# The first batch's k: transposed in float32 by TensorE instead of being cast to bf16 first, with a new instruction order

## The chip, the cores and the metric

The kernel runs on one core of one Trainium2 chip. A core has five engines that work side by side, each through its own queue in order: TensorE (PE in the profile, with its weight loads listed apart as PEld), VectorE (DVE), ScalarE (ACT), GpSimd (POOL) and SyncE (SP, which here only issues DMA transfers). Engines wait for one another by semaphores. PE reads its operands from SBUF and writes to PSUM, which has eight banks of 128 x 512 float32; the other engines copy the results out. The metric is the device time of one execution in microseconds (us), as the median of several runs. The cost of one instruction is best read from the distance between starts of neighbours, since the printed duration of a matmul or a copy contains a part that overlaps with the next.

## The reference: linear attention by random features, then a gated MLP

Inputs are q, k, v of shape (8 batches, 8 heads, 576 rows, 64), omega (128, 64), and two weights, w_in (512, 2048) and w_out (2048, 512), all float32. Cut to what is computed:

```python
def phi(x):                                   # x is q or k, scaled by 64 ** -0.25
    h = x @ omega.T - (x * x).sum(-1, keepdims=True) / 2
    return np.exp(h - h.max(-1, keepdims=True)) / np.sqrt(128)
q_p, k_p = phi(q), phi(k)                     # (8, 8, 576, 128)
kv  = einsum('bhsm,bhsd->bhmd', k_p, v)       # (8, 8, 128, 64)
z   = k_p.sum(2)
out = einsum('bhsm,bhmd->bhsd', q_p, kv) / (einsum('bhsm,bhm->bhs', q_p, z) + 1e-6)
x   = out.transpose(0, 2, 1, 3).reshape(4608, 512)
h   = x @ w_in                                # (4608, 2048)
y   = (h * clip(h + 3, 0, 6) / 6) @ w_out     # (4608, 512), float32
```

The kernel leaves out the factors that cancel between numerator and denominator: for k it divides the rows of v by the row maximum of the exponential, for q nothing is needed.

## The kernel before

**The work.** Attention goes batch by batch (`attention(b)`), heads in four pairs. Each of a batch's 576 rows splits into 512 main rows and 64 leftover rows. For a batch: transpose k and q so that the 64 features lie on partitions (`kT`, `qT`), project with omega on PE, take the exponential on ACT (`kp` for k, `qpT` for q), reduce a row maximum of `kp` on DVE (`mx`), invert it (`cc`), scale v by it (`vc`, `vcl`), multiply (`kv`, and its copy `kvz`), multiply with q's features (`num`), divide on DVE (`rec`, `div`) into `xb`, and transpose that into `xT` for the MLP. The MLP goes in blocks of 512 rows: `mm1` with w_in, the gate (a ReLU with scale and bias on ACT into `tsb`, then a minimum and a product on DVE into `gT`), `mm2` with w_out. Later blocks replace eight products by seven, with sums of operands made on POOL and DVE (names S, T, X, W). Block 0 runs through `mm1_half` in halves of 256 rows, each PE instruction group taking two of the sixteen feature groups of 128; its group 12 is the first to need the last quarter of w_in.

**The first batch.** Its rows of q, k, v are loaded as float32 by SP, with two of the k loads on ACT's queue. The main rows of k come in four pieces (two groups of head pairs, two heads of a pair). In the kernel before, each piece is cast to bf16 (`cast`: on ACT one piece, on POOL three) into `kb`; four PE transposes of 128 x 128 against a bf16 identity turn it into a PSUM bank (`turns`), and ACT or DVE copies 512 columns of bf16 out into `kT`. q is handled the same way. For batch 1 the load itself casts, on POOL's queue; from batch 2 on, DMA transposes.

**Filler.** So that PE is busy from the beginning, `idle_work` makes up to 76 matmuls of 256 columns that compute nothing (`fill`). The first 16 wait only for a memset; the others also for the first piece of k's main rows. The planner puts them where it sees PE idle, until 21 us of its own time.

**The order.** Nothing is scheduled on the chip. Every operation is recorded with `op(...)`: engine or choice of engines, a cost, reads and writes. The list `ORDER` at the head of the file gives, for each engine, the sequence of operations; it comes from a search outside the kernel, with a model of costs. `Prog.schedule` follows it, gives out PSUM banks and places the fillers; `Prog.emit` adds the semaphore waits. So an engine works strictly in the listed order, and a late operand stops what is queued behind it. The loads of w_in (five, cast to f16 by the DMA) and of w_out go through POOL's queue together with those of batch 1; SP's loads of v for batch 1 wait for the last piece of w_in.

**Lines.** In the profile of before, L571 fills the filler's operand and L576 is a filler matmul; L535 a transpose of k or q, L538 one of `xb`; L523 and L524 are copies and casts (523 on ACT, 524 on DVE and POOL); L811 projects k, L818 its exponential, L822 `mx`; L831 projects q, L835 its exponential; L850 and L935 invert the maximum; L941 and L943 make `vc` on POOL and on ACT, L857 and L860 `vcl`, L948 and L949 a column of `vc`; L957 and L959 are `kv`; L985 and L911 `num`, L997 and L1001 the division; L1199, L1054, L1133 and L1224, L1312 are matmuls of the MLP, L1208 and L1060 its ReLU, L1210 and L1062 its gate, L1328 sums out of PSUM; L622 loads q, k, v, and L595 and L604 load w_in and w_out.

Of the kernel before, what the change touches and what calls it, by code (L numbers as in the profile page):

```python
# [20 lines left out]
        13, 118, 139, 156, 124, 144, 150, 162, 115, 168, 147, 127, 153, 121, 159, 165, 136, 130, 133, 177, 185, 175,  # L21
        183, 197, 187, 142, 212, 179, 181, 199, 204, 214, 171, 227, 242, 202, 217, 229, 244, 219, 410, 416, 173, 189,
        417, 232, 404, 254, 247, 405, 222, 234, 406, 207, 249, 407, 257, 411, 412, 418, 413, 419, 422, 280, 425, 252,
        237, 260, 428, 300, 431, 434, 437, 440, 286, 284, 282, 443, 318, 306, 303, 288, 446, 449, 309, 312, 452, 298,
        296, 455, 315, 324, 294, 345, 458, 290, 575, 292, 321, 353, 576, 577, 327, 341, 335, 585, 586, 337, 339, 587,
        595, 588, 596, 331, 605, 366, 333, 578, 329, 579, 597, 355, 589, 590, 379, 598, 591, 368, 371, 592, 392, 580,
        581, 343, 606, 599, 381, 358, 607, 384, 600, 582, 394, 397, 601, 374, 608, 361, 609, 602, 387, 400, 610, 611,
        612, 638, 514, 626, 506, 629, 512, 623, 641, 632, 653, 504, 508, 499, 647, 644, 662, 656, 659, 484, 475, 487,
        496, 478, 481, 674, 668, 520, 518, 490, 493, 677, 510, 516, 671, 784, 785, 528, 502, 794, 533, 540, 530, 787,
        545, 542, 800, 564, 552, 788, 717, 554, 795, 569, 566, 557, 797, 798, 697, 801, 803, 804, 710, 807, 808, 811,  # L30
        817, 826, 724, 820, 737, 814, 832, 841, 829, 835, 739, 742, 749, 844, 847, 850, 761, 862, 856, 859, 773, 754,
        865, 778, 766, 751, 972, 988, 775, 973, 763, 982, 975, 976, 983, 885, 985, 986, 989, 898, 991, 992, 1005, 999,
        1014, 1002, 995, 996, 1017, 905, 1008, 1023, 1020, 1029, 925, 1035, 1032, 912, 1038, 1044, 937, 1050, 927,
        1047, 949, 1053, 939, 942, 930, 1160, 1161, 1176, 954, 961, 1170, 966, 951, 963, 1163, 1171, 1086, 1164, 1173,
        1174, 1073, 1177, 1179, 1180, 1093, 1202, 1193, 1190, 1187, 1183, 1184, 1100, 1205, 1196, 1113, 1208, 1217,
        1211, 1118, 1220, 1223, 1125, 1226, 1115, 1137, 1127, 1235, 1130, 1139, 1238, 1232, 1142, 1149, 1241, 1348,
        1349, 1151, 1364, 1154, 1351, 1274, 1352, 1358, 1359, 1281, 1365, 1361, 1362, 1390, 1375, 1378, 1381, 1367,
        1368, 1393, 1371, 1372, 1384, 1405, 1261, 1399, 1414, 1396, 1420, 1411, 1408, 1426, 1301, 1313, 1429, 1303,
        1318, 1306, 1536, 1315, 1423, 1325, 1537, 1288, 1552, 1539, 1540, 1327, 1546, 1330, 1547, 1462, 1337, 1549,
        1342, 1339, 1550, 1553, 1469, 1555, 1556, 1476, 1559, 1560, 1449, 1563, 1569, 1566, 1572, 1581, 1501, 1593,  # L40
        1506, 1503, 1489, 1584, 1525, 1494, 1578, 1491, 1530, 1527, 1513, 1587, 1518, 1596, 1515, 1599, 1602, 1614,
        1608, 1611, 1617, 1631, 1632, 1662, 1675, 1634, 1665, 1691, 1678, 1667, 1635, 1680, 1704, 1670, 1694, 1641,
        1720, 1696, 1683, 1642, 1707, 1699, 1723, 1709, 1733, 1644, 1645, 1725, 1712, 1749, 1736, 1650, 1738, 1728,
        1762, 1752, 1651, 1741, 1754, 1809, 1765, 1647, 1648, 1812, 1767, 1822, 1757, 1654, 1814, 1655, 1770, 1825,
        1817, 1838, 1827, 1778, 1779, 1841, 1851, 1830, 1843, 1867, 1781, 1854, 1782, 1846, 1856, 1880, 1870, 1788,
        1872, 1859, 1883, 1789, 1885, 1909, 1875, 1794, 1896, 1791, 1792, 1888, 1899, 1795, 1912, 1901, 1941, 1914,
        1797, 1798, 1904, 1917, 1801, 1935, 1925, 1926, 1802, 1936, 1928, 1929, 1938, 1939, 1942, 1960, 1957, 1945,
        1946, 1954,
    ],
    "SP": [  # L50
        0, 21, 17, 23, 19, 22, 25, 24, 31, 27, 32, 26, 28, 29, 30, 269, 270, 271, 474, 473, 472, 471, 470, 468, 690,
        469, 402, 614, 584, 694, 696, 594, 693, 695, 692, 604, 536, 548, 560, 572, 691, 573, 881, 878, 810, 883, 879,
        806, 745, 757, 781, 769, 882, 782, 880, 884, 1069, 998, 1072, 1066, 1070, 1071, 994, 1068, 933, 945, 970, 957,
        969, 1067, 1260, 1259, 1257, 1258, 1186, 1133, 1121, 1145, 1157, 1182, 1254, 1158, 1256, 1255, 1374, 1370,
        1447, 1445, 1446, 1448, 1309, 1443, 1333, 1321, 1345, 1444, 1346, 1442, 1509, 1497, 1533, 1521, 1562, 1558,
        1534, 1653, 1657, 1800, 1804, 1953, 1952, 1959, 1962, 1950, 1956,
    ],
    "ACT": [
        18, 20, 117, 119, 157, 145, 151, 163, 132, 169, 148, 129, 154, 193, 166, 196, 160, 178, 211, 184, 137, 176,
        186, 225, 182, 180, 243, 188, 172, 218, 174, 190, 223, 408, 414, 420, 423, 281, 426, 238, 208, 429, 253, 432,  # L60
        301, 435, 438, 441, 283, 285, 444, 261, 319, 307, 304, 447, 310, 450, 313, 289, 299, 352, 297, 325, 346, 316,
        453, 291, 293, 354, 322, 328, 342, 336, 338, 456, 340, 332, 378, 367, 334, 391, 330, 459, 390, 380, 344, 593,
        583, 362, 375, 388, 401, 613, 507, 515, 630, 627, 624, 513, 642, 633, 639, 654, 505, 509, 500, 648, 645, 603,
        663, 657, 660, 476, 497, 482, 479, 485, 675, 488, 494, 519, 669, 491, 523, 511, 672, 517, 503, 529, 539, 678,
        521, 551, 550, 553, 565, 720, 718, 723, 722, 706, 703, 704, 700, 708, 698, 403, 713, 711, 716, 715, 736, 709,
        812, 702, 748, 818, 747, 729, 821, 727, 815, 725, 730, 827, 833, 830, 836, 759, 842, 848, 845, 851, 863, 857,
        774, 860, 866, 974, 977, 897, 894, 891, 896, 892, 888, 886, 899, 890, 903, 921, 901, 1000, 1006, 1003, 923,
        1015, 1018, 906, 936, 904, 1009, 1024, 908, 1021, 911, 1030, 910, 1036, 1033, 913, 574, 915, 1039, 1045, 918,
        938, 1051, 1048, 917, 1054, 959, 960, 962, 1091, 1087, 1092, 1089, 1079, 1084, 1076, 1082, 1074, 1078, 1080,
        1085, 1098, 1099, 1094, 1096, 1194, 1191, 1108, 1203, 1188, 1112, 1111, 1206, 1103, 1197, 1105, 1101, 1209,  # L70
        1212, 1124, 1136, 1218, 1221, 1106, 1224, 1126, 1227, 1138, 1147, 1148, 1239, 1233, 1236, 1242, 1350, 1277,
        1280, 1279, 1275, 1284, 1287, 1282, 1376, 1353, 1379, 1391, 1382, 1286, 1312, 1394, 1385, 1406, 1262, 1270,
        1268, 1266, 1400, 1264, 1415, 1267, 1397, 1297, 1412, 1273, 1409, 1272, 1427, 1324, 1421, 1323, 1430, 1538,
        1424, 1293, 1291, 1289, 1541, 1336, 1294, 1338, 1468, 1465, 1463, 1467, 1474, 1472, 1470, 1159, 1475, 1479,
        1477, 1482, 1481, 1450, 1452, 1458, 1456, 1564, 1455, 1570, 1567, 1454, 1488, 1573, 1502, 1461, 1582, 1460,
        1490, 1585, 1526, 1579, 1514, 1594, 1588, 1597, 1603, 1600, 1609, 1615, 1612, 1618, 1633, 1663, 1664, 1676,
        1677, 1666, 1692, 1679, 1671, 1693, 1636, 1673, 1695, 1684, 1705, 1706, 1686, 1722, 1708, 1700, 1724, 1702,
        1713, 1734, 1735, 1715, 1750, 1737, 1729, 1731, 1753, 1763, 1742, 1764, 1744, 1758, 1810, 1813, 1823, 1760,
        1771, 1824, 1773, 1826, 1818, 1820, 1839, 1831, 1842, 1780, 1852, 1853, 1847, 1833, 1783, 1849, 1860, 1881,
        1882, 1862, 1884, 1876, 1878, 1897, 1889, 1891, 1900, 1913, 1905, 1918, 1907, 1920, 1927, 1930, 1948, 1949,  # L80
        1951,
    ],
    "DVE": [
        16, 12, 11, 15, 14, 5, 138, 4, 9, 140, 10, 125, 7, 158, 146, 116, 191, 152, 164, 6, 122, 128, 149, 155, 194,
        209, 134, 167, 170, 131, 161, 141, 239, 224, 198, 143, 200, 213, 201, 205, 215, 216, 228, 203, 206, 230, 245,
        231, 220, 246, 221, 233, 255, 248, 235, 236, 250, 258, 256, 251, 409, 415, 259, 421, 424, 8, 427, 1623, 430,
# [316 lines left out]
def _emit(nc, es, q, k, v, omega, w_in, w_out, out):  # L403
# [38 lines left out]
    def sbt(name, shape, dt):  # L442
        return es.enter_context(nc.sbuf_tensor(name, list(shape), dt))
# [166 lines left out]
    def mains_of(t):  # L610
        return t[:, NP:, :].rearrange("p (m h r) d -> p m h (r d)", h=2, r=4)
# [890 lines left out]
```

The softmax here doesn't subtract the row's maximum and nothing guards it: scores larger than these inputs give would overflow.

## Time and profile before

| | us |
|---|---|
| median of six runs | 303.89 (303.27 to 304.55) |
| the profiled execution's own time | 304.24 |
| its span, from first to last instruction | 302.40 |
| PE busy in the span | 295.75 |
| PE busy from 0 to 22 us, filler included | 19.73 |
| first real MLP matmul (L1199) | 20.6 |
| DMA, mean over the span | 148 GB/s |

The profiled execution took 0.35 us more than the median, and 1.84 us lie outside its span. In the profile, a line of the timeline gives start, length, engine, source line, operation and tiles, `xN` for N merged instructions, and in brackets the idle time before it with the engine or DMA that ended it. "Busy" for PE counts pipelined matmuls as they overlap, so 98% says that PE is rarely without an instruction, not that each is useful.

### The profile page before, as it was taken

What the parts mean: (1) busy time and instruction counts of PE and PEld (TensorE: products, weight loads), DVE (VectorE), ACT (ScalarE), POOL (GpSimd) and SP (SyncE); (2) the same over time, 40 slices, a digit from 0 to 9 for tenths busy, and PEclk for the clock granted to TensorE, in tenths of its full rate; (3) what the DMA queues carried; (4) which work ended last, traced back from release to release, by engine and by line L of the source; (5) the groups of instructions that cost most, each with busy time, mean ns of one, the idle gap of its engine ahead of it and who ended that gap; (6) DMA issues with size and microseconds to landing.
All of it is one profiled execution on the core that took longest, in us unless ns stands there. A gap on an engine that the chain in (4) does not pass through costs nothing.

```text
span 302.4 us, 7405 instructions
## 1 busy us (share of the span) xinstructions
PE 295.8 (98%) x2795; PEld 211.4 (70%) x2800; DVE 246.4 (81%) x547; ACT 214.2 (71%) x516; POOL 237.8 (79%) x255
## 2 busy tenths in 40 slices
PE   7999999999999999999999999999999999999995
PEld 5779955545776568655865586657756688888884
DVE  3889887859988794879878967687798999999875
ACT  4898996579949963799479854697686687575400
POOL 2883776069896999799969996998959999999990
PEclk9999999999999999999999999999999999999999
DMA  7999999999996996799949969797832500110034
GB/s 236 285 194 185 267 180 110 195 179 149 233 196 113 143 235 169 159 157 234 181 107 137 160 158 236 107 223 132 138 90 52 168 1 2 69 73 2 0 141 140
DMA packets 90100, 44.89 MB, mean 148 GB/s; under 512 B 57936, under 2 KB 87760, under 8 KB 90064
## 3 DMA queue, kind: packets, MB, share of 16 engines
q1 hardware_dynamic: 62496, 31.04, 45.4%
q0 software_dynamic: 26592, 12.46, 33.4%
q10 hardware_dynamic: 976, 0.92, 0.9%
q8 instruction: 22, 0.36, 0.5%
q14 instruction: 14, 0.11, 0.2%
HBM read 36.73 MB, written 9.44 MB: 153 GB/s over the span
## 4 chain that ended last, share of the span: by engine, by line
PE 87%; ACT 7%; DVE 5%; issue 0%
PE p L1312 32%; PE p L1054 24%; PE p L1133 8%; PE p L1224 5%; PE p L985 3%; PE p L1199 3%; PE p L957 3%; PE p L767 2%; ACT kp L818 2%; DVE gT L1062 2%; PE p L770 2%; PE p L576 1%; DVE mx L822 1%; ACT qpT L835 1%; PE p L831 1%; ACT tsb L1060 1%
## 5 line engine op out<-in xcount | busy, mean ns | idle before, releaser
L1054 PE MATMUL p<-xT,wi 128*128 128x512 f16 x384 | 89.9, 379 | 0.1
L1062 DVE SCALAR_TENSOR_TENSOR gT<-tsb,p 128x512 f16<-128x512 f16 x96 | 62.2, 676 | 12.8 <-ACT tsb L1060 12.2
L1060 ACT ACTIVATE tsb<-p 128x512 f16<-128x512 f32 x96 | 55.4, 606 | 14.7 <-PE p L1054 8.9
L1054 PEld LDWEIGHTS p<-xT,wi 128*128 128x128 f16 x384 | 35.7, 98 | 38.5 <-issue 1.1
L1312 PE MATMUL p<-wo,gT 128*128 128x256 f16 x368 | 45.3, 273 | 0.0
L1240 POOL TENSOR_TENSOR gT<-gT 128x512 f16<-128x512 f16 x32 | 36.9, 1155 | 3.2 <-DVE gT L1062 0.9
L1312 PEld LDWEIGHTS p<-wo,gT 128*128 128x128 f16 x368 | 35.0, 98 | 6.4 <-issue 1.1
L1240 POOL TENSOR_TENSOR s<-gT 128x512 f16<-128x512 f16 x31 | 36.2, 1168 | 3.9 <-DVE gT L1062 1.7
L1240 POOL TENSOR_TENSOR s<-gT,s 128x512 f16<-128x512 f16 x31 | 35.9, 1157 | 2.6 <-DVE gT L1062 0.3
L1240 POOL TENSOR_TENSOR gT<-gT,s 128x512 f16<-128x512 f16 x30 | 34.7, 1155 | 2.3
L791 DVE TENSOR_REDUCE mx<-kp 128x4 f32<-128x512 bf16 (+1 forms) x50 | 29.7, 621 | 6.5 <-ACT kp L786 6.4
L795 ACT ACTIVATE qpT<-p 128x512 bf16<-128x512 f32 (+1 forms) x50 | 27.5, 570 | 7.7 <-PE p L770 7.1
L622 POOL DMA_DIRECT2D qb<-in_q_dram x28 | 19.6, 716 | 16.7 <-PE p L1054 15.8
L1312 PE MATMUL p<-t,gT 128*128 128x256 f16 x256 | 31.6, 273 | 0.0
L786 ACT ACTIVATE kp<-p 128x512 bf16<-128x512 f32 (+1 forms) x50 | 26.2, 568 | 7.5 <-PE p L770 7.5
L941 POOL TENSOR_TENSOR vc<-v,cc 128x512 bf16<-128x512 f32 x22 | 24.0, 1089 | 8.8 <-DMA v<-in_v_dram 3.6
L1001 DVE TENSOR_TENSOR xb<-p,rec 128x256 f16<-128x256 f32 (+1 forms) x64 | 28.4, 470 | 0.3
L1312 PEld LDWEIGHTS p<-t,gT 128*128 128x128 f16 x256 | 24.4, 98 | 4.5 <-issue 1.6
L523 ACT COPY p<-p 128x256 f32<-128x256 f32 (+1 forms) x42 | 16.4, 402 | 14.9 <-PE p L1312 8.6
L1181 ACT ACTIVATE tsb<-p 128x512 f16<-128x512 f32 x32 | 18.7, 601 | 8.3 <-PE p L1133 6.2
L1183 DVE SCALAR_TENSOR_TENSOR gT<-tsb,p 128x512 f16<-128x512 f16 x32 | 21.1, 678 | 0.5 <-ACT tsb L1181 0.3
L943 ACT ACTIVATE vc<-v,cc 128x64 bf16<-128x64 f32 x80 | 20.2, 345 | 0.0
(132 smaller groups left out, 583.7 us busy)
## 6 DMA issues: line engine op xcount, KB each, us to landing
v<-in_v_dram SPq DMA_DIRECT2D x14, 512.0 KB, 5.4
out_dram<-osb SPq DMA_DIRECT2D x14, 512.0 KB, 3.7
kb<-in_k_dram POOLq DMA_DIRECT2D x14, 256.0 KB, 5.2
qb<-in_q_dram POOLq DMA_DIRECT2D x14, 256.0 KB, 5.9
wo<-in_moe_w_out_dram POOLq DMA_DIRECT2D x8, 256.0 KB, 9.5
wi<-in_moe_w_in_dram POOLq DMA_DIRECT2D x3, 512.0 KB, 7.4
q<-in_q_dram SPq DMA_DIRECT2D x4, 256.0 KB, 5.3
v<-in_v_dram SPq DMA_DIRECT2D x4, 256.0 KB, 5.6
```

The source lines that it names most:

```text
L786: op("ACT", actt(128 * (d1 - d0)), lambda E, lh=lh, ko=ko, part=part: E.activation(ko, out_of(part, 0, lh)[0].rearrange("p (x m) -> p x m" ...
L791: op("DVE", dvet(128 * (d1 - d0)), lambda E, ko=ko, mo=mo: E.reduce_max(mo, ko, axis=AX.X), p0 + 0.01, reads=[("kp", 0, d, lh) for d in ra ...
L795: op("ACT", actt(128 * (d1 - d0)), lambda E, lh=lh, part=part: E.activation(qd[:, part[0]:part[1], lh, :], out_of(part, 1, lh)[0].rearrang ...
L941: return E.tensor_tensor(vcm[:, :, 0:D], v32[:, m, :, :], cbc, ALU.mult)
L1001: op("DVE", dvet(128 * n), lambda E: E.tensor_tensor(xv(i0, i1), psum()[:, :, :, 0:64], rbc, ALU.mult), t + 0.01, reads=[vn, ("rec", ru)], ...
L1054: ins = E.matmul(ring.t[vh.slot], wi[:, c, 128 * f:128 * f + 128], xv[:, c, :], start=(c == 0), stop=(c == NJ - 1))
L1060: op("ACT", actt(512), lambda E: E.activation(tsb[tu][:], ring.t[vh.slot], AF.Relu, bias=0.5, scale=1.0 / 6.0), t - 0.1, reads=[vh], write ...
L1062: op("DVE", dvet(512), lambda E: E.scalar_tensor_tensor(gT[gu][:, f, :], tsb[tu][:], 1.0, ring.t[vh.slot], ALU.min, ALU.mult), t - 0.1, re ...
L1133: ins = E.matmul(dst, w(c), x[:, c, :], start=start and c == 0, stop=c == 1, skip_group_check=True)
L1183: op("DVE", dvet(512), lambda E, v=v, tu=tu, dst=dst: E.scalar_tensor_tensor(dst(), pieces(tsb[tu][:]), 1.0, pieces(v.ring.t[v.slot]), ALU ...
L1240: op(engines, {"POOL": 0.07 + n / 455.0, "DVE": 0.1 + n / 850.0}, lambda E: E.tensor_tensor(dst, x, y, ALU.subtract if minus else ALU.add) ...
L1312: ins = E.matmul(ring.t[v.slot][:, 256 * j:256 * j + 256], a[:, f, 128 * j:128 * j + 128], w[:, f, :], start=(first and f == 0 and j == 0) ...
```

## The change

The four casts of k's main rows in batch 0 are gone. PE transposes the float32 rows directly, against a float32 copy of the identity (a new 128 x 128 tile, made by one POOL copy), into a whole PSUM bank of float32. The copy out of PSUM writes bf16, so it does the rounding that the cast did. k's leftover rows and all of q still go through the cast. `ORDER` is replaced as a whole by a new sequence; the planner's rule for placing fillers is the same, and with the new sequence it places 49 instead of 65.

```diff
 ORDER = {
...
-    (five sequences)
+    (five other sequences)
...
     ident = sbt("ident", [128, 128], BF16)
+    identf = sbt("identf", [128, 128], F32)
...
+    op("POOL", 0.3, lambda E: E.tensor_copy(identf[:], ident[:]), -8.95, reads=["ident"], writes=["identf"])
     op("POOL", 0.3, lambda E: E.tensor_copy(identx[:], ident[:]), -8.9, reads=["ident"], writes=["identx"])
...
+        def turns32(t, name, dbl, dst, src, rd, p):
+            vT = Virt(ring)
+            n = 128 * len(dbl)
+
+            def e_T(E):
+                for i, x in enumerate(dbl):
+                    ins = E.transpose(ring.t[vT.slot][:, 128 * i:128 * i + 128],
+                                      src[:, 2 * x:2 * x + 2, :].rearrange("p c d -> p (c d)"), identf[:])
+                return ins
+
+            op("PE", len(dbl) * 0.23, e_T, p, reads=rd + ["identf"], writes=[vT], alloc=[vT], lat=0.25, name="T%s%d.%s" % (t, b, name))
+            op(T0, both(n), evac(lambda: dst, lambda: ring.t[vT.slot][:, 0:n].rearrange("p (j t) -> p j t", j=dst.shape[1])),
+               p, reads=[vT], writes=[(t + "T", x) for x in dbl], name="Tev%s%d.%s" % (t, b, name))
+
...
                 for hh in range(2):
                     nm = "%d%d" % (m0 // 2, hh)
                     dbl = four(m0, m1, hh)
-                    cast("k", nm, 512, mains_of(kb)[:, m0:m1, hh, :], mains_of(k32)[:, m0:m1, hh, :],
-                         main_keys("k", range(m0, m1), [hh]), dbl, 0)
-                    turns("k", nm, dbl, dbls(kT)[:, m0:m1, hh, :], kb, 0)
+                    turns32("k", nm, dbl, dbls(kT)[:, m0:m1, hh, :], k32, main_keys("k", range(m0, m1), [hh]), 0)
```

What the new sequence moves near the start, beside the change itself: `vc` of head pair 2 goes from ACT to POOL, the cast of k's leftover rows from DVE to POOL, one cast of q's main rows from ACT to DVE and that of q's leftover rows from DVE to ACT; on SP one k load comes one place later and one v load ahead of a q load; on POOL the first three loads of w_in are issued one after another. Later on, single copies and sums of the MLP change between ACT, DVE and POOL and change places.

## The prediction

> **What bounds the kernel now.** I read the page first: engines, slices, shares of the chain.
>
> ```profile
> PE 295.8 (98%) x2795; PEld 211.4 (70%) x2800; DVE 246.4 (81%) x547; ACT 214.2 (71%) x516; POOL 237.8 (79%) x255
> ...
> PE   7999999999999999999999999999999999999995
> ...
> PE 87%; ACT 7%; DVE 5%; issue 0%
> ```
>
> TensorE (PE) is the bound everywhere but in the first slices and the last. Much of its early "work" is filler (L576). Second, PE's timeline of 0 to 22 us shows where the filler ends and what the clock does.
>
> ```profile
> 1.19 2.74 PE L576 MATMUL p<-fill 128*128 128x256 bf16 x12 [1.19 <-DVE fill L571]
> 3.72 0.31 PE L561 MATMUL p<-ident,om 128*128 128x128 bf16 x1
> ...
> 4.68 0.96 PE L535 MATMUL p<-ident,kb 128*128 128x128 bf16 x6
> 5.99 0.59 PE L811 MATMUL p<-om,kT 128*128 128x256 bf16 x2 [0.34 <-DVE kT L524]
> ...
> 11.28 0.83 PE L535 MATMUL p<-ident,qb 128*128 128x128 bf16 x12
> 11.95 0.38 PE L831 MATMUL p<-qT,om 128*128 128x512 bf16 x1
> 12.16 1.04 PE L576 MATMUL p<-fill 128*128 128x256 bf16 x8
> ...
> 20.23 0.27 PE L576 MATMUL p<-fill 128*128 128x256 bf16 x1
> 20.34 0.41 PE L985 MATMUL p<-kvz,qpT 128*128 128x65 bf16 x8
> ```
>
> Start-to-start gives prices: a 256-column matmul costs (3.72-1.19)/12 = 0.211 us at first and about 0.109 later (8 in 0.88 from 12.16 to the next start, 13.04); a bf16 transpose (11.95-11.28)/12 = 0.056; a 512-column matmul 0.21. Filler ends for good at 20.34. Third, the waits of PE over the whole span:
>
> ```profile
> PE p L576 <- DVE fill L571: 1.2, 1, 1.2
> PE p L957 <- ACT qT L523: 0.5, 1, 0.5
> PE p L576 <- ACT kp L818: 0.4, 1, 0.4
> PE p L1312 <- DVE u L1328: 0.4, 1, 0.4
> ```
>
> After 20.34 two real stops are left: 0.69 us between starts at 41 us (listed 0.5) and 0.51 at 87 us (listed 0.4), with 0.1 elsewhere: 1.3 us. So a change can win what it takes from the start, plus at most 1.3 us. Last, ACT's, SP's and PE's timelines around two places:
>
> ```profile
> 3.87 0.62 ACT L523 CAST kb<-k 128x512 bf16<-128x512 f32 x1 [0.82 <-DMA k<-in_k_dram]
> ...
> 6.61 2.06 ACT L818 ACTIVATE kp<-p 128x512 bf16<-128x512 f32 x4 [0.68 <-PE p L811]
> ...
> 17.03 2.04 ACT L943 ACTIVATE vc<-v,cc 128x64 bf16<-128x64 f32 x8
> ```
> ```profile
> 27.60 0.37 SPq L622 DMA_DIRECT2D vl<-in_v_dram  x1
> ```
> ```profile
> 27.55 0.38 PE L811 MATMUL p<-om,kT 128*128 128x256 bf16 x2
> 27.77 3.66 PE L1199 MATMUL p<-xT,wi 128*128 128x256 f16 x32
> ```
>
> The SP load at 27.60 is gated on the last quarter of w_in (columns 1536 on), so that quarter landed just before. The matmul group at 27.77 is the first that reads it. It starts with 0.17 us to spare.
>
> **The change, part by part.** All sums run against the profiled execution (304.24 us, 302.40 of span); the median of the six runs is 0.35 lower.
>
> *Casts out.* Four 512-element casts of k go: three on POOL (0.61 each), one on ACT (0.5 of spacing). POOL sat idle for k then (5.1 us over three waits), so its 1.8 us are worth nothing; ACT's 0.5 shortens ACT's list. The identity copy added on POOL (the 0.29 of `identx`, now both before 3 us) hides in POOL's idle 3.71 us before its first cast.
>
> *Transposes in float32.* Sixteen. No row shows one. Lower end: the bf16 row, 0.056 (0.107 at the early half speed). Upper end: the dearest matmul there is, 512 columns, 0.215 (0.43 early). A float32 transpose is nearer to the bf16 row in shape and to the 512 row in bits moved; I take the upper end, the cautious one: 16 x (0.215-0.056) = 2.5 us more PE work, all where there is filler now.
>
> *Copies out of PSUM.* kT now comes from float32. On ACT 512 elements cost 0.49 of spacing either way. On DVE the bf16 copy took 0.41 and the float32 copy of 512 (L524, `osb`) 0.69: two stay there, +0.56 us in the first 10 us, while DVE waits 1.3 us for ACT (its `mx` wait at 12.7).
>
> *Order.* 49 fillers instead of 65; `vc` of pair 2 from ACT (1.9 us) to POOL (1.05); the cast of k's leftover rows from DVE to POOL, one cast of q from ACT to DVE, q's leftover cast from DVE to ACT. On SP, `k01` goes back one place (each place is 0.75 us by the waits that end at 6.21 and 7.78, two apart), a v load goes ahead of `q01`, and q's leftover loads go behind it. On POOL, the loads of w_in are issued in one run from 9.47, the third to land at about 12 instead of 12.92, and the fourth about 2.5 us earlier than 15.82; the fifth moves from 20.19 to about 20.6, since `vc` comes first.
>
> *Start, worked along the new order.* 16 fillers: 1.19 + 16 x 0.2135 = 4.60. The first four float32 transposes wait for nothing (their rows of k landed by 3.87): 4 x 0.43 = 1.71, to 6.31. Drain 0.2 and DVE copy 0.6: 7.1. The copies of omega and two memsets behind it (0.29+0.28+2 x 0.11): 7.8. Meanwhile PE does eight more (1.8 us, full clock from about 6.5) and two bf16: 8.4. So the first projection is at 8.4, the first exponential at 8.85, 2.2 us later than 6.61. From there ACT binds: 9 exponentials of k and 8 of q at 0.49, one of 256 at 0.28, one kT copy 0.49, casts 0.28+0.52, `vcl` 1.05, four small 0.1: 11.35 us, and 0.15 of waiting: 20.35; the last filler (it needs ACT's slot) ends near 20.55. In the cheap case the first exponential is at 7.1, then ACT waits 1.1 us for q's rows: near 19.95. By then the new order has done 0.54 us more matmuls (0.22+0.11+2 x 0.11) than the old one at 20.34. Gain: 20.34+0.54-20.55 = 0.33, or 0.93 if cheap.
>
> *What is late next.* Up to the group at 27.77 both orders do the same PE work, so the group would come 0.33 (0.93) earlier. But w_in's last quarter lands at 27.6 unless DMA gets faster: the share is above 1.0 in every window from 5 to 30 us, the bytes ahead of it are the same, and an earlier issue only lengthens the 7.2 us from issue to landing (ends: 0 gained if DMA binds, 0.4 lost if its issue does). So the start is worth 0.17 us in both cases.
>
> *Rest of the span.* Same instructions in another order. Its stops lie between 0 and, by what one shuffled stretch can cost (next part), about 3 us; I take 0.2 more than the present 1.3, because two stops in 280 us is an order that can hardly improve. The tail after the last matmul has the same instructions. Sum: -0.17+0.2 = 0.0: 304.2 for the profiled execution, 303.9 for the median.
>
> [...] In this trace six bf16 transposes ran from 4.68 and spacing still halved by 6.5. [...]
>
> **The rivals.**
>
> *Float32 transposes dearer than a 512-column matmul (slower).* Place: before the first exponential, with ACT behind it. It counts four at half clock and eight at full, 16 full-clock prices. At 0.43 full clock, twice my price (each with its own unhidden weight load, 0.1 to 0.15 per PEld row, several times), the first exponential is 3.45 us later; less 0.33 that is 3.1: 307.0. It decides above about 0.215+(0.33+0.9)/16 = 0.29. For: no row; against: filler still stands there, and nothing says more than 512 columns' worth.
>
> *More stops between 60 and 90 us (slower).* There the chain leaves PE for 12.8 us (62.35 to 75.17 is ACT and DVE alone) and DVE is busy 9.97 of 10 us from 70 to 80. The new order shuffles the weight sums (1024 elements, 0.7 to 1.3 us each) and `gT` (0.68) there, and the copies that free PSUM. Two of them on the wrong side of a needed one: +1.4 to 2; 305.5. Against: DVE's work there is the same in sum.
>
> *The stops vanish (faster).* Both stops at 41 and 87 hang on one instruction each (an ACT copy, a DVE sum); another order may have none: -0.17-1.3 = -1.5; 302.4. If the w_in quarter landed earlier as well, -2.2. Against: two stops would have to go and none come.
>
> **How the numbers follow.** No change 0.45 (303.0 to 304.8, around 303.9), dear transposes or slow clock 0.16, more stops 0.22, stops gone 0.17. The bound of 0.3% is 0.9 us, about what this kernel's runs can tell from no change. So faster 0.17, same 0.45, slower 0.38. Range 302.7 to 306.1: it leaves out the best half of the faster case (0.07) and the dear end of the transposes with the worst of the stops (0.12).
>
> **What would show it.** The spacing of the transposes (0.215 at full clock) and whether it halves near 6.5; first exponential near 8.85; last filler near 20.55; the gated SP load still at 27.6 and PE stopped before the group that now stands at 27.77, 0.1 to 0.2 us (up to 0.8 if cheap); PE waits after that of about 1.5 us. I am wrong if w_in's quarter lands elsewhere, if the transposes cost over 0.29, or if PE waits in 40 to 90 us come to 2 us or to nothing.

## The result, and the profile after

The changed kernel takes 306.4 us (median of 19 runs, 304.23 to 310.12) against 303.94 us for the kernel before (38 runs, 303.18 to 305.75). The ratio is 1.0073, with a 95% interval of 1.0054 to 1.0093: slower, by more than the 0.3% (0.9 us) that the prediction takes as the bound of "no change". The ratios in this document are of fast runs alone (18 of these 19; the one of 310.12 is left out), so they differ a little from the quotient of the medians; 1.0073 is 2.2 us. The prediction was 303.9 and its range ended at 306.1, so the result is outside. The spread is news too: 6 us from best to worst, where the kernel before has under 3.

The profiled execution of the changed kernel is one of its quick ones: 304.93 us, of which 303.0 us are span, 0.6 us more than the span before. First the page (engines, and shares of the chain that ended last):

```profile
PE 295.3 (97%) x2780; PEld 210.3 (69%) x2784; DVE 246.0 (81%) x541; ACT 215.5 (71%) x522; POOL 235.0 (78%) x253
...
PE 79%; POOL 6%; ACT 5%; SPq 3%; DMA 3%; issue 2%; DVE 1%; POOLq 0%; ACTq 0%
```

PE is still the bound. What is new is the last line: POOL, SP's queue and DMA, which had no share of the chain before, now hold 12%. That does not cost anything by itself, but it says that in this execution POOL and transfers set part of the pace. Then PE's timeline of the start (start, length, engine, line, operation, tiles; in brackets the idle time before it and what ended it):

```profile
4.36 0.60 PE L703 MATMUL p<-identf,k 128*128 128x128 f32 x4
4.80 0.22 PE L563 MATMUL p<-ident,om 128*128 128x128 bf16 x1
...
6.82 0.66 PE L703 MATMUL p<-identf,k 128*128 128x128 f32 x4 [0.84 <-DMA k<-in_k_dram]
...
20.91 0.42 PE L578 MATMUL p<-fill 128*128 128x256 bf16 x2
21.21 0.30 PE L999 MATMUL p<-kvz,qpT 128*128 128x65 bf16 x4
...
28.19 3.00 PE L1213 MATMUL p<-xT,wi 128*128 128x256 f16 x26
```

Four float32 transposes take 0.44 us, 0.109 each. Filler ends at 21.21 (20.34 before), and the group that needs the last quarter of w_in starts at 28.19 (27.77 before). PE's waits over the whole span, and ACT's and SP's rows that answer to those shown of before:

```profile
PE p L578 <- DVE fill L573: 1.2, 1, 1.2
PE p L703 <- DMA k<-in_k_dram: 1.0, 2, 0.8
...
PE p L536 <- DVE qb L525: 0.4, 1, 0.4
PE p L1326 <- DVE u L1342: 0.4, 1, 0.4
```
```profile
7.73 1.08 ACT L832 ACTIVATE kp<-p 128x512 bf16<-128x512 f32 x2 [1.24 <-PE p L825]
```
```profile
27.88 0.37 SPq L624 DMA_DIRECT2D v<-in_v_dram  x1
```

In this execution the stop at 41 us is gone, the one at 87 us (0.51 between starts) is still there, and the stops after the last filler sum to 1.4 us, against 1.3 before. Nothing here costs 2.2 us. The group of 28.19 is late by 0.4 us, most of the 0.6 us of difference between the two spans. So the loss should lie in executions that look different, and one place in this profile is a near miss. On SP and on ACT, in the stretch where batch 4 (counted from 0) takes over:

```profile
115.66 4.08 SPq L1044 DMA_TRANSPOSE xT<-xb  x3
119.78 2.36 SPq L901 DMA_TRANSPOSE xs<-xb  x1
122.19 0.58 SPq L624 DMA_DIRECT2D vl<-in_v_dram  x1
122.81 1.06 SPq L624 DMA_DIRECT2D v<-in_v_dram  x2
```
```profile
128.26 2.02 ACT L957 ACTIVATE vc<-v,cc 128x64 bf16<-128x64 f32 x8 [0.53 <-issue]
```

The same two views of the kernel before:

```profile
109.89 0.53 SPq L622 DMA_DIRECT2D v<-in_v_dram  x1
...
120.87 1.26 SPq L887 DMA_TRANSPOSE xs<-xb  x1
122.17 0.58 SPq L622 DMA_DIRECT2D v<-in_v_dram  x1
```
```profile
128.47 2.02 ACT L943 ACTIVATE vc<-v,cc 128x64 bf16<-128x64 f32 x8
```

Before, batch 4's v comes in two loads, one issued at 109.89 and one at 122.17. (The leftover rows were loaded earlier, at 105.61.) The second took 4.3 us from issue to landing, so v is in by 126.5, and ACT turns to it at 128.47: 2.0 us to spare. In the new sequence all three loads (the leftover rows `vl.4` and the main loads `v00.4`, `v10.4`) stand behind the xs transpose. The last is issued at 123.4 and lands 4.8 us later, at 128.2. ACT comes sooner: one ReLU (`tsb`) that stood ahead of this `vc` now stands behind it, and `vcl` (1.05 us) has moved to POOL. ACT was free at 127.73. So v is late by half a microsecond, although the row puts the 0.53 us down to "issue". Behind that `vc` on ACT stands an exponential (`kp`) that PE will turn out to wait for.

### The profile page after: what moved, and what is told of

The parts are those of the page before. It is cut to its first block, busy times and chain, and to the rows that moved or that the text cites. A ratio compares the mean times of both kernels' runs of the same rounds, so it can differ in the third digit from the quotient of the medians.

```text
span 303.0 us, 7358 instructions
## 1 busy us (share of the span) xinstructions
PE 295.3 (97%) x2780; PEld 210.3 (69%) x2784; DVE 246.0 (81%) x541; ACT 215.5 (71%) x522; POOL 235.0 (78%) x253
## 4 chain that ended last, share of the span: by engine, by line
PE 79%; POOL 6%; ACT 5%; SPq 3%; DMA 3%; issue 2%; DVE 1%; POOLq 0%; ACTq 0%
PE p L1326 29%; PE p L1068 23%; PE p L1147 8%; PE p L1238 4%; POOL s L1254 3%; PE p L999 3%; PE p L971 2%; PE p L781 2%; DMA q<-in_q_dram 2%; SPq L624 2%; PE p L1213 2%; ACT tsb L1222 2%; PE p L845 1%; PE p L784 1%; DMA v<-in_v_dram 1%
## 5 line engine op out<-in xcount | busy, mean ns | idle before, releaser
L1254 POOL TENSOR_TENSOR s<-gT 128x512 f16<-128x512 f16 x30 | 35.0, 1168 | 3.5 <-DVE gT L1076 1.4
L955 POOL TENSOR_TENSOR vc<-v,cc 128x512 bf16<-128x512 f32 x21 | 22.5, 1071 | 13.1 <-DMA v<-in_v_dram 7.2
L524 ACT COPY p<-p 128x256 f32<-128x256 f32 (+1 forms) x46 | 18.2, 405 | 8.2 <-PE p L1147 4.2
L957 ACT ACTIVATE vc<-v,cc 128x64 bf16<-128x64 f32 x88 | 22.2, 348 | 0.7 <-issue 0.5
```

Of the source, the lines that this page charges most:

```text
L955: return E.tensor_tensor(vcm[:, :, 0:D], v32[:, m, :, :], cbc, ALU.mult)
L1254: op(engines, {"POOL": 0.07 + n / 455.0, "DVE": 0.1 + n / 850.0}, lambda E: E.tensor_tensor(dst, x, y, ALU.subtract if minus else ALU.add) ...
```

## The experiments

All kernels were timed beside the kernel before on the same chip, in three sets (before: 304.27, 304.34 and 304.08 us). Edits of `ORDER` are shown with the names of operations in place of their numbers. On SP, `vl.4`, `v00.4` and `v10.4` are the loads of batch 4's v (the "fifth batch" of the expectations); `Xdma`, `Sdma`, `Tdmak` and `Tdmaq` are DMA transposes, of xT, of xs (the leftover rows of `xb`), of k and of q; `outw` is an output store.

### First set: which part of the change?

Two halves of the change (the float32 transposes, the sequence) and two halves of the sequence, cut at the group of PE that needs the last quarter of w_in (about 28 us).

```diff
 f32_old_order: the changed kernel with the sequence of before
 ORDER = {
-    (new sequence)
+    (sequence of before, without the four casts of k, with the copy of the identity)
```


> The float32 transposes alone, in the sequence of before (the four casts dropped, the float32 identity added, everything else in its old place). Theory F (the transposes themselves, or the clock behind them, cost the time): about +2.4 us against before, as the whole change. Theories S and R (the new sequence costs it, in its first 28 us or after them): within 0.5 us of before, since a float32 transpose took 0.109 between starts at full clock and 16 of them are 0.85 us more where filler stood.

Measured: 304.49 us, ratio 1.0011 (0.9993 to 1.0028). The float32 transposes alone make no difference that these runs can tell. PE's timeline, in a part where the clock was still at half (three fillers took 0.64 us from 3.83 to 4.47, 0.213 each; five from 7.31 took 0.55, 0.11 each):

```profile
4.47 1.06 PE L693 MATMUL p<-identf,k 128*128 128x128 f32 x4
5.32 0.42 PE L568 MATMUL p<-fill 128*128 128x256 bf16 x1
```

Four in 0.85 us is 0.213 each at half clock, twice the 0.107 of bf16, as 0.109 at full clock is twice 0.056.

```diff
 cast_new_order: the kernel before (casts in) with the new sequence
 ORDER = {
-    (sequence of before)
+    (new sequence, with the four casts where their engines are free)
```


> The new sequence with the old casts put back (bf16 transposes). Theory F: back to before, within 0.5 us. Theories S and R: still 2 to 3 us slower than before.

Measured: 306.97 us, 1.0095 (1.0059 to 1.0131). The sequence is slow with the casts too, but not for one reason: its profile has a wait of PE for w_in at 28.6 us (1.7 us between starts) that the profiles of the changed kernel have not; that the casts do not fit into the new start is the likely cause, not a shown one. So this run does not size the loss of the sequence; the next two do. Its ACT has the late v:

```profile
PE p L1190 <- DMA wi<-in_moe_w_in_dram: 1.5, 1, 1.5
```
```profile
131.10 2.02 ACT L934 ACTIVATE vc<-v,cc 128x64 bf16<-128x64 f32 x8 [1.05 <-DMA v<-in_v_dram]
```

```diff
 new_start_old_rest: the changed kernel; each engine's list
 ORDER = {
     (new sequence up to mm1.0A.12 on PE)
-    (new sequence)
+    (sequence of before for all that is left)
```


> The changed kernel up to the first matmul group that needs the last quarter of w_in (27.8 us in before), and the old sequence for all that comes after. Theory S (the new start loses it: q and k rows that land later, PE stops in front of them): 2 to 3 us slower than before and as spread as the changed kernel. Theory R: 0.4 us slower, the lag of that group in the profiles (28.19 against 27.77).

```diff
 old_start_new_rest: the kernel before; each engine's list
 ORDER = {
     (sequence of before up to mm1.0A.12 on PE)
-    (sequence of before)
+    (new sequence for all that is left)
```


> The old start with casts up to the same group, and the new sequence after it. Theory S: within 0.5 us of before. Theory R: about 2 us slower than before. Theory F: within 0.5 us of before.

Measured: the new start with the old rest 304.18 us, 1.000 (0.9975 to 1.0025); the old start with the new rest 306.14 us, 1.0066 (1.0037 to 1.0095). The start is worth nothing in either direction, and the loss is made after 28 us. The profile of the second shows one stop that is not in before. ACT's row, then PE's:

```profile
129.17 2.02 ACT L934 ACTIVATE vc<-v,cc 128x64 bf16<-128x64 f32 x8 [2.13 <-DMA v<-in_v_dram]
```
```profile
132.20 1.47 PE L1045 MATMUL p<-xT,wi 128*128 128x512 f16 x6 [1.30 <-ACT kp L777]
```

From here the theory V: v of batch 4 is late for ACT. Its rivals: W, many small stops all over the new sequence; L, a loss after 142 us.

### Second set: moving the loads, and cutting the rest in two

```diff
 after_v4_ahead: the changed kernel, SP's list
-    Tdmaq.4.1, outw.1.1, Xdma.3.1, Xdma.3.2, Xdma.3.3, Sdma.3, vl.4, v00.4, v10.4,
+    Tdmaq.4.1, vl.4, v00.4, outw.1.1, Xdma.3.1, Xdma.3.2, Xdma.3.3, Sdma.3, v10.4,
```


> The changed kernel with two SP entries moved: the left-over load vl.4 and the first main load v00.4 of the fifth batch's v go ahead of the three last xT transposes of the block before, where the kernel before has them; the second main load v10.4 stays behind the xs transpose. V (the loss is the fifth batch's v, landing at 128.2 us just when ACT's queue reaches its first vc at 128.3, so that every execution in which it lands later stops ACT and then PE): v10.4 is issued 1.2 us earlier, the wait of ACT for v goes, ratio to before 0.999 to 1.003, and no execution above 307. W (many small stops strewn over the new sequence): ratio stays at 1.005 to 1.009. L (the loss is made after 142 us): the same as W.

Measured: 305.89 us, 1.0062 (1.0037 to 1.0087). The expectation of V failed, and the profile says why: the edit did not bring v forward. The transposes behind the two loads ran later, and the last load (`v10.4`) was issued at 124.24, not earlier but 0.9 us later than in the changed kernel (123.36). It took 4.4 us and landed at 128.7; ACT had been free since 127.31. SP's row, that load's landing, and ACT's row:

```profile
124.24 0.58 SPq L615 DMA_DIRECT2D v<-in_v_dram  x1
```
```profile
DMA to landing us min/median/max: 4.4/4.4/4.4
```
```profile
128.74 2.02 ACT L948 ACTIVATE vc<-v,cc 128x64 bf16<-128x64 f32 x8 [1.43 <-DVE mx L796]
```

ACT's row names a maximum on DVE, but `vc` reads v and `cc` only, and the `cc` that it reads was done at 126.06; the maximum merely ended at the same moment. ACT waited for v here too. PE waited twice, for a late xT transpose and, as elsewhere, for ACT's exponential behind `vc`:

```profile
PE p L1059 <- DMA xT<-xb: 0.9, 1, 0.9
PE p L1059 <- ACT kp L791: 0.6, 1, 0.6
```

The edit left one transfer late and made another late, so its time cannot tell V from W. Its profile has the late v and PE's stop behind it, as V says.

```diff
 before_v4_behind: the kernel before, SP's list
-    Tdmak.4.0, vl.4, outw.1.0, Tdmaq.4.0, v00.4, outw.1.1, Xdma.3.0, ..., Tdmak.4.1, Sdma.3, v10.4, Tdmaq.4.1,
+    Tdmak.4.0, outw.1.0, Tdmaq.4.0, outw.1.1, Xdma.3.0, ..., Tdmak.4.1, Sdma.3, vl.4, v00.4, v10.4, Tdmaq.4.1,
```


> The kernel before with the same two SP entries moved the other way: vl.4 and v00.4 go behind the xT and xs transposes of their block, ahead of v10.4, as in the changed kernel. V: v10.4 is issued about a microsecond later, ACT waits for v at its first vc of the fifth batch (128.5 us) by 0 to 3 us depending on the landing, PE follows with a stop at about 130; ratio 1.004 to 1.009 and a spread of several us. W and L: ratio 0.998 to 1.002.

Measured: 305.26 us, 1.0029 (1.0001 to 1.0058), up to 308.38. Slower, by less than V said. ACT does wait for v now, 0.86 us, which is too little for a stop of PE at 130. What PE does wait for is the q transpose behind the loads, and a `vc` of POOL (POOL itself stood 3.57 us for that q transpose). ACT's row and PE's waits:

```profile
128.94 2.02 ACT L933 ACTIVATE vc<-v,cc 128x64 bf16<-128x64 f32 x8 [0.86 <-DMA v<-in_v_dram]
```
```profile
PE p L947 <- POOL vc L939: 1.1, 1, 1.1
PE p L757 <- DMA qT<-qb: 0.9, 1, 0.9
```

Both edits say the same of SP here: in the changed kernel three loads and nine transposes stand in one queue between 106 and 126 us, and in both edits what was put ahead made later ones late.

```diff
 new_to_p3_old: the changed kernel; each engine's list
 ORDER = {
     (new sequence up to the first product of mm2 of block 3, P3.0, about 142 us)
-    (new sequence)
+    (sequence of before for all that is left)
```


> The changed kernel's sequence on every engine up to the products of the fourth block (about 142 us), the old sequence after it. V: the whole loss is in, ratio 1.005 to 1.009, single executions up to 310. L: 0.999 to 1.002. W: half of the loss, 1.002 to 1.005.

```diff
 old_to_p3_new: the kernel before; each engine's list
 ORDER = {
     (sequence of before up to P3.0)
-    (sequence of before)
+    (new sequence for all that is left)
```


> The old sequence (with the casts) up to the products of the fourth block, the new one after it. V: 0.999 to 1.002. L: 1.005 to 1.009. W: half of the loss, 1.002 to 1.005.

Measured: 308.08 us, 1.0116 (1.0072 to 1.016), and 307.9 us, 1.0115 (1.0082 to 1.0149). No theory expected both halves to lose more than the whole. The first half has the late v, worse than elsewhere (ACT's row):

```profile
130.53 2.02 ACT L947 ACTIVATE vc<-v,cc 128x64 bf16<-128x64 f32 x8 [3.29 <-DMA v<-in_v_dram]
```

The second has no late v. Its profile has two stops where the sequences were joined: ACT was given a copy, `kvz` and a `vc` of 2 us one behind the other, and PE waited for two of them:

```profile
PE p L976 <- ACT kvz L514: 1.0, 1, 1.0
PE p L948 <- ACT vc L939: 0.8, 1, 0.8
```

The cut in the middle of a running pipeline made a loss of its own, 2.1 us between starts. This run cannot speak for L or against it, and a loss at the cut is not excluded for the first half either.

### Third set: one SP entry, forward and back

The next edits move the loads across a single SP entry. Ahead of it, they pass the xs transpose, whose data is first used at 140.8 us in the first profile of the changed kernel (the expectation has 136); behind it, an output store.

```diff
 after_v4_before_xs: the changed kernel, SP's list
-    Xdma.3.3, Sdma.3, vl.4, v00.4, v10.4, outw.2.1,
+    Xdma.3.3, vl.4, v00.4, v10.4, Sdma.3, outw.2.1,
```


> The changed kernel with the three v loads of the fifth batch (vl.4, v00.4, v10.4) moved ahead of one SP entry alone, the xs transpose of the block before, whose data is first used at 136 us. They are issued 1.3 to 2.4 us earlier, no xT transpose and no output store ahead of them moves. V (ACT's first vc of that batch stops ACT whenever v lands after 128.3 us): no wait of ACT for v at 128 us and no PE stop at 130 to 132; ratio 1.000 to 1.004, median at least 1 us under that of the unchanged changed kernel of this set. W (loss made elsewhere in the new sequence): same median as the unchanged one, 306 to 307, ratio 1.006 to 1.009.

```diff
 after_v4_later: the changed kernel, SP's list
-    Sdma.3, vl.4, v00.4, v10.4, outw.2.1, Tdmaq.5.0,
+    Sdma.3, vl.4, outw.2.1, v00.4, v10.4, Tdmaq.5.0,
```


> The changed kernel with the two main v loads of the fifth batch moved behind one SP entry more, the output store outw.2.1, which starts at 125.7 us: the loads are issued 2.5 to 3 us later. V: ACT waits for v by 2 to 4 us in every execution, PE stops for 2 us or more at 130 to 132, median 308 to 311 and a granted clock of 0.994 in part of the executions. W: v still has room, 306 to 307.

```diff
 after_again: the changed kernel, no edit
```


> The changed kernel, unchanged, as the yardstick of this set and for a second profile: 305.5 to 307, ratio 1.005 to 1.009 by all theories. V: a profile of an execution above 306 has the wait of ACT for v at 128 us and a PE stop of 1.5 us or more near 131; one near 304.5 has none. W: the longer execution has its time in other places.

Measured: ahead of xs 304.72 us, 1.0022 (0.9996 to 1.0048); as it is 305.98 us, 1.0060 (1.0037 to 1.0083); one entry later 311.94 us, 1.026 (1.0234 to 1.0287). Two thirds of the loss go with one entry of one queue; the two intervals overlap, so the 0.38% between them is only just clear of noise. The opposite move costs 6 us, far outside it, and more than V had said (308 to 311). The profile of the unchanged kernel is now of a slower execution (306.6 us). Its rows of ACT and PE:

```profile
129.61 2.02 ACT L957 ACTIVATE vc<-v,cc 128x64 bf16<-128x64 f32 x8 [2.56 <-DMA v<-in_v_dram]
```
```profile
132.64 1.90 PE L1068 MATMUL p<-xT,wi 128*128 128x512 f16 x8 [1.73 <-ACT kp L800]
```

The loads were issued at the same time as in the first profile (122.87 for 122.81). This time v took 6.1 us to land. The chain through that place, in order of time (start, length, what):

```profile
118.13 0.70 DVE u L1342
118.83 2.08 SPq L1044
...
120.95 1.25 SPq L901
...
122.87 0.51 SPq L624
...
123.42 6.12 DMA v<-in_v_dram
...
129.61 2.02 ACT vc L957 x8
```

A DVE sum is the last input of the xT transpose; xT, xs, `vl` and two loads follow on SP without a gap; and ACT stands until the last has landed. With the loads ahead of xs they start at 120.76. The rows of SP, the landing of the last load (issued at 121.93), and ACT's row:

```profile
120.76 0.58 SPq L615 DMA_DIRECT2D vl<-in_v_dram  x1
121.38 1.06 SPq L615 DMA_DIRECT2D v<-in_v_dram  x2
```
```profile
DMA to landing us min/median/max: 5.8/5.8/5.8
```
```profile
127.84 2.02 ACT L948 ACTIVATE vc<-v,cc 128x64 bf16<-128x64 f32 x8 [0.77 <-issue]
```

ACT's row names no DMA, but ACT was free at 127.06 and v landed at 127.8. So the wait that V said would go is still there, 0.77 us of it; the load was issued 1.4 us earlier than in the changed kernel and took 5.8 us instead of 4.8 or 6.1. What went is PE's stop: 0.1 us is left.

One entry later the last load took 7.6 us, ACT waits 6.49 us, PE 5.66, and the clock follows (the page's slice of granted clock, 7.75 us each):

```profile
133.39 2.02 ACT L948 ACTIVATE vc<-v,cc 128x64 bf16<-128x64 f32 x8 [6.49 <-DMA v<-in_v_dram]
```
```profile
136.43 1.89 PE L1059 MATMUL p<-xT,wi 128*128 128x512 f16 x4 [5.66 <-ACT kp L791]
```
```profile
PEclk9999999999999999969999999999999999999999
```

Put side by side, the profiles with the new sequence at this place give one rule. PE's stop, measured between starts, is ACT's wait less 0.67 us. In the first five ACT's row names the DMA; in the other two it names something else, but there too `vc` starts within 0.1 us of the landing of v:

| kernel | ACT waits for v | PE's stop | difference |
|---|---|---|---|
| cast_new_order | 1.05 | 0.38 | 0.67 |
| old_start_new_rest | 2.13 | 1.47 | 0.66 |
| after_again | 2.56 | 1.90 | 0.66 |
| new_to_p3_old | 3.29 | 2.62 | 0.67 |
| after_v4_later | 6.49 | 5.82 | 0.67 |
| after_v4_before_xs | 0.77 | 0.10 | 0.67 |
| after_v4_ahead | 1.43 | 0.76 | 0.67 |

It also fits the first profile of the changed kernel: ACT's 0.53 us there is below 0.67, and PE did not stop. So a late v costs PE nothing up to 0.67 us, and all that lies above it.

```diff
 old_start_v4_before_xs: old_start_new_rest, SP's list
-    Xdma.3.3, Sdma.3, vl.4, v00.4, v10.4, outw.2.1,
+    Xdma.3.3, vl.4, v00.4, v10.4, Sdma.3, outw.2.1,
```


> The kernel with the old start (with the casts) and the new sequence behind it, which took 306.1 us, with the same three v loads ahead of the xs transpose. V: 303.0 to 304.7, ratio 0.997 to 1.001. W: 306, ratio 1.005 or more.

Measured: 305.16 us, 1.0037 (1.0012 to 1.0063), where the same kernel without the edit had 1.0066 in the first set. Lower, but above what V expected. In its profile ACT's `vc` waits for nothing, so the late v is gone here; 0.6 us between starts are lost at 27.8 us to w_in, where the old start meets the new rest, and two stops of 0.25 to 0.29 us stand near 114 and 118 us. About a third of a per cent (1.1 us) stays, half of it at that join in this profile; the rest is open, and W is not excluded for it.

No kernel of these beats the kernel before.

## Why the prediction was wrong

**The step that failed is "Rest of the span":** "I take 0.2 more than the present 1.3". The start was worked through row by row for 20 us. The 275 us behind it got one sentence and a guess, although both sequences could be read. In its place the runs showed a stop of PE at 131 us that before does not have, from 0 to 2.6 us long, 1.9 in the slower profile of the changed kernel. The right step would have compared, for each load, its place on SP with the place of its first user. For batch 4's v the rows of before nearly give it. Its last load moves behind two more (0.58 and 0.53 us), so it is issued at about 123.3 instead of 122.2 and lands 4.3 to 4.8 us later, at 127.6 to 128.1. ACT wants it up to 1.5 us earlier, since one `vcl` (1.05) and one `tsb` (0.48 of spacing) no longer stand ahead: at 127.0 or somewhat later. That is a wait of up to 1.1 us, at a place where before had 2.0 us of room. By the 0.67 us found above it would stop PE for 0.4 us at most. So the sign could be read; the rest of the size needs landings of 5.5 to 6.1 us, which the rows of before do not show.

**The rival "more stops" was the right kind at the wrong place.** It gave 305.5 us, with DVE at 60 to 90 us as the cause. There the new sequence has 0.8 us of stops in the profile of after. The stop that decides is at 131 us, made by a transfer and passed on by ACT.

**How the size comes out.** The slower profile of the unchanged kernel has a span of 304.6 us against 302.4: 2.2 us, of which 1.90 are that stop. For the 2.2 us of those 18 runs, an estimate from the profiles: the stop was 0, 0.38, 1.47, 1.90 and 2.62 us in five profiles whose order is the new one at this place, 1.3 us in the mean. Three of the 18 have a mean granted clock of 0.994 where the profiled one has 1.000; 0.006 of about 307 us is 1.8 us, as if the clock had been at half for 3.7 us. That costs at most 1.8 us each, 0.3 in the mean. None of those three was profiled, so this part is argued. With it, 1.6 of 2.2 us are named; the edit that moves the loads took away 1.26 us of 1.9 in its own set. The 0.6 us that are left in it are within its interval of nothing.

**The float32 transposes were mis-sized, and it did not matter.** Priced at 0.215 us, the upper bound, they cost 0.109: 0.85 us of extra PE work for sixteen instead of 2.5. The first exponential came at 7.73, between the 8.85 of the sum and the 7.1 of the cheap case. Yet the last filler ended at 21.21, later than both (20.55 and 19.95): PE waited 0.84 us for the third piece of k and 0.4 for q's cast, which itself waited for q's rows. The sum had q's rows only as a wait of ACT in the cheap case.

**"The start is worth 0.17 us in both cases" was near in size by luck.** The start bought nothing (new start with old rest: 1.000), but not because w_in capped it. The gated SP load started at 27.88, 27.48 and 27.05 us in three profiles with the new start (after, after_again, after_v4_before_xs), and the group followed at 28.19, 27.79 and 27.99, without a stop of PE before it. PE came to that group late by itself, since the start had gained nothing.

**"No change", at 0.45, was what the transposes and the start gave; it left out the one thing that the new sequence did.** The rival "the stops vanish" was half right: the 0.69 us at 41 us went, the 0.51 at 87 stayed.

**The clock during the transposes.** The chances count a slow clock, together with dear transposes, at 0.16. No run shows transposes that keep the clock at half; the runs show it going to full while PE transposed. The slower profile of the changed kernel:

```profile
4.58 1.06 PE L703 MATMUL p<-identf,k 128*128 128x128 f32 x4
5.43 0.31 PE L563 MATMUL p<-ident,om 128*128 128x128 bf16 x1
5.54 1.06 PE L703 MATMUL p<-identf,k 128*128 128x128 f32 x4
6.39 0.42 PE L536 MATMUL p<-ident,kb 128*128 128x128 bf16 x2
6.60 0.87 PE L703 MATMUL p<-identf,k 128*128 128x128 f32 x4
7.30 0.82 PE L825 MATMUL p<-om,kT 128*128 128x256 bf16 x6
```

The first two groups of four took 0.85 us each between starts, 0.213 a transpose: half clock. The third took 0.70; at 0.213 and 0.109 a piece that is two and a half at half clock, which puts the rise at 7.14 us (an estimate from these rows). Filler had stood until 4.58; from there to 7.14 PE did nothing but transposes and one matmul of 128 columns (L563), and the clock rose all the same. In the first profile it rose at 4.13, after 2.94 us of filler (four fillers from 3.72 took 0.64 us, two at half clock and two at full). What sets the moment is not shown.

## What to carry to other kernels

When a sequence is searched anew, the instruction that the change names is the smaller part of it: list every load's place in its queue against the place of its first user, before and after, and look for room that went from positive to about zero. Such a place need not show in one profile, since a quick execution just makes it; here a spread that grew from 3 to 6 us in 19 runs pointed to it, though the six runs of after_again lay within 1.2 us. To mend it, move the load across one entry whose own user is far off; the moves across many entries made other transfers late, and one of them the last load itself. And check the name in a wait's bracket against the landing: three rows here named "issue" or DVE where the trace shows that v had just landed.

## What the runs showed of the hardware that was not expected

- The last of the same two v loads, issued at the same time, landed 4.8 us after issue in one execution of the changed kernel and 6.1 us in another; issued 1.4 us earlier it took 5.8, and 2.4 us later 7.6. A room below the 1.3 us between the first two did not hold in both.
- A float32 transpose of 128 x 128 takes 0.109 us at full clock and 0.213 at half, twice the bf16 one in both.
- A stop of PE of 5.8 us was followed by half clock (after_v4_later): the eight matmuls of 512 columns behind it took 3.38 us between starts, 0.42 each, where they took 1.74 behind the stop of 1.90 us in after_again; with the `kv` behind them PE needed 3.94 us for 2.06, 1.9 us more. The mean granted clock of 0.989 over a span of 310.0 us is worth about 6.8 us at half (an estimate). Stops of 2.62 us and less, after 30 us, left the clock at full in the profiles: behind that of 2.62 the eight took 1.74 us.
